# A GFNet token mixer and a SiLU feed-forward block in one kernel: row stores moved from ScalarE's queue to SyncE's, the last rows fetched group by group, one batch's first input laid on 128 partitions, its results stored before other stores, and the weight conversion cut into other pieces

## The chip, the cores and the metric

The kernel runs on one core of one Trainium2 chip. The metric is the device time of one execution in microseconds. Three runs of the kernel before took 2512.32, 2512.67 and 2513.15 us; the median is 2512.67 us.

The core has five engines, each with its own queue that is worked off in order: TensorE (PE, matmuls), VectorE (DVE), ScalarE (ACT), GpSimd (POOL) and SyncE (SP, which here only issues DMAs). DMAs are issued from the queues of SP, ACT and POOL. An engine that waits for a semaphore holds up everything behind it in its queue.

## The reference

```python
x: (8, 3008, 256)            # batch, tokens, channels
X = rfft(x, axis=1)          # over the tokens
y = irfft(X * F, n=3008)     # F = filt_r + i filt_i, per frequency and channel
h = y.reshape(24064, 256) @ w_in      # 256 -> 2048
out = silu(h) @ w_out                 # 2048 -> 256, silu(h) = h / (1 + exp(-h))
```

x, F and out are float32; w_in and w_out arrive as float64 and are turned into float32 on the core.

## The kernel before, in words

**The feed-forward part** makes up nearly all of the time. The tokens are worked off in 48 *pairs* of blocks, each with 8 *steps*: 384 steps in all. A step multiplies a pair's tokens with one 256-column slice of w_in (`hidden`), applies SiLU, and the step after multiplies the result with the matching slice of w_out (`project`). Both products use Strassen's scheme: seven matmuls in place of eight, for which sums of weights (S1, S2, S3, S4) stand beside the weight blocks A11, A12, A22. One step holds up to eight *rounds*. In its rounds `hidden` emits the matmuls A11 (round 0), A12 (1), S2 (2), S1 (3), S3 (4), A22 (6) and S4 (7); between them `project` emits the seven matmuls of the step before. TensorE takes them in that order.

On VectorE a step leaves this sequence: `g0` (A12's sum, after the matmul A12), then `finish` (two sums of the step before), later `g2` (after S3), `g1` (after S4), and, after a SiLU of ScalarE on `g1`, the wide sum `g46`. VectorE works it off in exactly this order: g1, g46 of one step, then g0 of the next, then finish. ScalarE copies the results of A11, S2 and S3 out of PSUM (`abc`) and applies the four SiLUs.

The steps are ordered so: pair 0 with weight slices 0, 1, 2 (steps 0 to 2), pair 1 with slices 0 to 7 (steps 3 to 10), then the rest of pair 0. So slice 1 is first used in step 1, slice 2 in step 2, slice 3 in step 6, slices 4 to 7 in steps 7 to 10.

**The weights** are prepared on the core. For each of 16 raw tiles j (two for each slice): `weights` loads it (512 KB, SP), `bits` takes exponent and mantissa words apart (VectorE, two instructions), `converted` makes the new exponent (ScalarE, two), `added` adds the low word, `signed` puts the sign back, `placed` multiplies both into `w_t` (VectorE, one each). `combine_weights(slice)` then makes the four sums with four VectorE additions: the first two (part 0) make S1 and S2, the other two (part 1) S3 and S4. `rounded` is added and signed together.

**The spectral part** of a batch is a mixed-radix transform in three stages of small matmuls, with two trips through DRAM (`d1` after stage 1, `d2` after the inverse of the middle stage). Batch 0 has to be done before any feed-forward step can start, so the kernel begins with a prologue: load batch 0, stage 1 (L392), `forward` (L526), filter products on VectorE and POOL, six inverse groups (`inverse_first`, L660), each evicted into two tiles q (`rows_first`, L678). Each q tile holds two halves of the token residues; the first halves are stored to d2 at once (`store_half(g, i, 0, ...)`, L684), by ACT for groups 0 to 3 and one tile each of groups 4 and 5, by SP for the other two. `load_t4_rows(k)` (L711) fetches 16 of the 48 rows each: k = 0 and 2 by SP, k = 1 by POOL. `stage3` (L726) then makes the first half of batch 0's tokens, y[0, 0], and L740 evicts it. Meanwhile stage 1 of batch 1 begins: `load_two` loads the first two pieces of its x on 96 partitions, `stage1` (L416) multiplies them and ACT copies them into the tiles t1 (L421). While the PE has to wait in this stretch, matmuls without a use (`idle`) are run.

Once y[0, 0] is there, a small POOL copy (`gate`, L1374) opens a series of POOL DMAs: the twelve second halves of the q tiles (L684), and then the eight stores of batch 1's t1 tiles to d1 (`store_rows`, L429). The tiles t1 come from a pool of two buffers, so the next piece of stage 1 (t1 of piece 2, copied by ACT in step 1) has to wait until the first piece's four stores have landed. SP loads the later weights and pieces of x.

**What orders the rest**: `put(step, round, piece)` writes each other piece of work into the engines' queues at a place given by step and round. The long table near the end (L1395 and on) places the weights' pieces in steps 0 to 9, `plan` places the spectral work of batches 1 to 7.

## Time and profile before

| what | us |
|---|---|
| median of the runs | 2512.67 |
| the profiled execution, its own time | 2514.95 |
| its span, first to last instruction | 2513.0 |
| TensorE busy in the span | 2484.8 |
| VectorE busy | 1760.7 |
| ScalarE busy | 1095.1 |
| POOL busy | 438.4 |
| prologue, until the first matmul of step 0 | 59.80 |

The first matmuls (A11) of steps 0 to 11 start at 59.80, 65.05, 81.73, 90.63, 98.46, 107.42, 115.35, 123.77, 130.85, 138.09, 144.43 and 151.78 us; a step later in the kernel lasts a little over 6 us plus what spectral work is put into it. The profiled execution is 2.28 us longer than the median of the runs, and 1.95 us of its time lie outside the span.

A line of the timeline gives the start, the time until the end of the group, the engine, the line of the kernel, the operation, what is written and read, the count, and in brackets the idle time before it and who ended it. A line of the chain gives the start, the length and the work. A matmul of 256 columns in float32 shows as two instructions.

### The profile page before, as it was taken

What the parts mean: (1) busy time and instruction counts of PE and PEld (TensorE: products, weight loads), DVE (VectorE), ACT (ScalarE), POOL (GpSimd) and SP (SyncE); (2) the same over time, 40 slices, a digit from 0 to 9 for tenths busy, and PEclk for the clock granted to TensorE, in tenths of its full rate; (3) what the DMA queues carried; (4) which work ended last, traced back from release to release, by engine and by line L of the source; (5) the groups of instructions that cost most, each with busy time, mean ns of one, the idle gap of its engine ahead of it and who ended that gap; (6) DMA issues with size and microseconds to landing.
All of it is one profiled execution on the core that took longest, in us unless ns stands there. A gap on an engine that the chain in (4) does not pass through costs nothing.

```text
span 2513.0 us, 42305 instructions
## 1 busy us (share of the span) xinstructions
PE 2484.8 (99%) x16238; PEld 2127.2 (85%) x16238; DVE 1760.7 (70%) x3608; ACT 1095.1 (44%) x3006; POOL 438.4 (17%) x687
## 2 busy tenths in 40 slices
PE   8899999999999999999999999999999999999999
PEld 6678888888888888888888888888888888888988
DVE  6766777777777777777777767777677766655544
ACT  3544444444444444444444444444444444444443
POOL 3202212022121121210222112211122111101100
PEclk9999999999999999999999999999999999999999
DMA  7522242312333132420324203331042211200000
GB/s 256 191 72 90 65 101 52 87 51 67 73 72 83 35 80 60 100 71 19 93 58 111 60 26 77 86 74 43 26 107 62 55 43 34 63 21 9 17 9 17
DMA packets 139513, 170.67 MB, mean 68 GB/s; under 512 B 21084, under 2 KB 113084, under 8 KB 138684
## 3 DMA queue, kind: packets, MB, share of 16 engines
q1 hardware_dynamic: 115408, 120.23, 18.2%
q0 software_dynamic: 22816, 46.20, 7.0%
q8 instruction: 127, 2.08, 0.3%
q10 hardware_dynamic: 1088, 1.56, 0.2%
q14 instruction: 74, 0.61, 0.1%
HBM read 96.06 MB, written 81.26 MB: 71 GB/s over the span
## 4 chain that ended last, share of the span: by engine, by line
PE 96%; DVE 2%; DMA 1%; ACT 0%; issue 0%; POOL 0%; SPq 0%; DVEq 0%; ACTq 0%
PE acc L1057 45%; PE px L989 25%; PE pyz L989 19%; PE pd L764 1%; PE pf L486 1%; PE pc L582 1%; PE pb L544 1%; DVE g L960 1%; PE pc L660 0%; PE pa L392 0%; PE pd L726 0%; PE pb L526 0%; DMA d<-t 0%; DMA d<-q 0%; DMA w_t<-d 0%
## 5 line engine op out<-in xcount | busy, mean ns | idle before, releaser
L1057 PE MATMUL acc<-g,w_t 128*128 128x256 f32 (+1 forms) x5376 | 1508.5, 376 | 3.0 <-ACT o L777 2.5
L1057 PEld LDWEIGHTS acc<-g,w_t 128*128 128x128 f32 x5376 | 1016.6, 190 | 154.6 <-ACT o L777 15.3
L960 DVE TENSOR_TENSOR g<-pyz,abc 128x256 f32<-128x256 f32 (+1 forms) x1152 | 479.6, 416 | 481.5 <-ACT abc L1010 240.7
L960 DVE TENSOR_TENSOR g<-g 128x256 f32<-128x256 f32 (+3 forms) x1152 | 590.6, 513 | 196.6 <-ACT g L993 183.4
L989 PE MATMUL px<-ty,w_t 128*128 128x256 f32 (+1 forms) x2304 | 676.6, 375 | 7.7 <-ACT abc L1010 7.7
L993 ACT ACTIVATE g<-g 128x256 f32<-128x256 f32 (+1 forms) x1152 | 472.9, 411 | 241.5 <-DVE g L960 241.5
L989 PEld LDWEIGHTS px<-ty,w_t 128*128 128x128 f32 x2304 | 434.2, 190 | 65.4 <-ACT abc L1010 8.9
L960 POOL TENSOR_TENSOR s<-s 128x256 f32<-128x256 f32 (+1 forms) x322 | 246.3, 782 | 1387.3 <-DVE s L1083 1043.7
L989 PE MATMUL pyz<-y,w_t 128*128 128x256 f32 (+1 forms) x1536 | 452.4, 376 | 3.0 <-DVE g L960 2.6
L989 PEld LDWEIGHTS pyz<-y,w_t 128*128 128x128 f32 x1536 | 283.3, 189 | 49.0 <-DVE g L960 9.0
L1004 ACT COPY abc<-px 128x256 f32<-128x256 f32 (+1 forms) x384 | 141.4, 368 | 369.8 <-PE px L989 369.8
L1010 ACT COPY abc<-px 128x256 f32<-128x256 f32 (+1 forms) x384 | 141.5, 368 | 308.6 <-PE px L989 308.5
L993 ACT ACTIVATE g<-px 128x256 f32<-128x256 f32 (+1 forms) x384 | 145.8, 380 | 298.1 <-PE px L989 298.1
L989 PE MATMUL px<-y,w_t 128*128 128x256 f32 (+1 forms) x768 | 227.6, 378 | 0.5 <-ACT g L993 0.5
L989 PE MATMUL pyz<-ty,w_t 128*128 128x256 f32 (+1 forms) x768 | 225.6, 375 | 0.2 <-DVE g L960 0.2
L989 PEld LDWEIGHTS px<-y,w_t 128*128 128x128 f32 x768 | 143.8, 190 | 23.2 <-ACT g L993 2.2
L989 PEld LDWEIGHTS pyz<-ty,w_t 128*128 128x128 f32 x768 | 142.0, 190 | 21.5 <-DVE g L960 1.3
L997 ACT COPY abc<-px 128x256 f32<-128x256 f32 (+1 forms) x384 | 135.1, 352 | 35.5 <-PE px L989 35.5
L506 POOL DMA_DIRECT2D d<-tf x96 | 48.5, 505 | 215.8 <-DVE tf L436 212.9
L1083 ACT COPY s<-acc 128x512 f32<-128x512 f32 (+1 forms) x92 | 53.0, 577 | 46.4 <-issue 28.8
L603 POOL DMA_DIRECT2D d<-low x36 | 22.2, 618 | 289.1 <-DVE low L599 289.1
L476 DVE TENSOR_TENSOR uf<-x_all 120x512 f32<-120x512 f32 (+1 forms) x72 | 60.2, 864 | 0.0
(133 smaller groups left out, 1363.2 us busy)
## 6 DMA issues: line engine op xcount, KB each, us to landing
t<-d SPq DMA_DIRECT2D x84, 256.0 KB
t<-d SPq DMA_DIRECT2D x224, 96.0 KB
out_dram<-s SPq DMA_DIRECT2D x62, 256.0 KB
d<-q POOLq DMA_DIRECT2D x48, 256.0 KB, 5.2
x_all<-in_x_dram SPq DMA_DIRECT2D x96, 96.0 KB
x_all<-xr SPq DMA_DIRECT2D x96, 96.0 KB
d<-tf POOLq DMA_DIRECT2D x96, 96.0 KB, 2.7
d<-tq POOLq DMA_DIRECT2D x96, 96.0 KB, 2.8
```

The lines of the kernel that those rows point to most:

```text
L476: nc.vector.tensor_tensor(out=out, in0=in0, in1=in1, op=op)
L486: nc.tensor.matmul(out=ps[q][32 * k:32 * k + 32], lhsT=wq_t[rows, k], rhs=rhs[k][rows], start=True, stop=True)
L506: nc.gpsimd.dma_start(out=d1[par, :, grp, at:at + 4], in_=part[rows].rearrange("p q n c -> p (q n) c"))
L544: nc.tensor.matmul(out=ps[k, ri][32 * j:32 * j + 32, a, :], lhsT=dn_t[rows, 4 * (g + a) + at, :], rhs=t2s[g + a][rows, at, :], start=True, ...
L960: eng.tensor_tensor(out=out, in0=in0, in1=in1, op=op)
L989: nc.tensor.matmul(out=out, lhsT=w_t[:, jp, c, 0], rhs=rhs, start=start, stop=True, skip_group_check=True)
L993: nc.scalar.activation(out=g[:, k, 0:n], in_=g[:, k, 0:n] if src is None else src, func=AFT.Silu)
L997: nc.scalar.copy(out=sums[:, 0, 0:n], in_=xo)
L1004: nc.scalar.copy(out=sums[:, 1, 0:n], in_=xo)
L1010: nc.scalar.copy(out=sums[:, 2, 0:n], in_=xo)
L1057: nc.tensor.matmul(out=acc[pair][i][:, h, 0:n], lhsT=w_t[:, jp, OUT_PLACE.get(c, c), 1], rhs=g[:, k, 0:n], start=(new and h == 0), stop=la ...
L1083: copy(out=dst, in_=src)
```

## The change

1. **Row stores issued by SP.** Of the first-half stores, ACT issues one tile each of groups 0, 1, 2, 3 and 5; SP issues the other seven (five more than before). ACT now makes the copies of group 4 and one of group 5 with no issue between them.
2. **Last rows fetched by group.** `load_t4_rows` becomes `fetch_rows(a0, n, queue)`; the last 16 rows are fetched by SP in two portions of eight (rows 32 to 39 of group 4, then 40 to 47 of group 5), four DMAs of 128 KB in place of two of 256 KB.
3. **Batch 1's first x on 128 partitions.** `load_four` loads it in four DMAs onto 32 partitions each, with a contraction of three blocks of 32 rows; `stage1_four` multiplies it with twelve matmuls on four row groups in place of four on 96 rows. One of the four copies moves to VectorE. The table wx3 gets a tile of its own in another pool. The idle matmuls change from 24 small and 6 large ones to 9 and 12.
4. **t stored ahead of the halves.** The eight `store_rows` DMAs come before the twelve second halves in POOL's queue.
5. **The weights' pieces.** In the prologue, `added(0, 1)`, `bits(2, 3)` and `added(2, 3)` come earlier; tiles 7 to 10 are loaded in step 1. In the table, `rounded` is no longer used, combine_weights of slices 1, 2 and 3 is cut into its two parts, and the pieces move; the last one is in step 10 instead of step 9. One eviction of y (group 1) moves from ACT to VectorE, the token sums of pair 1 from round 3 to round 5 of step 2.

```diff
-        def load_two():
-            load_rows(x_all.rearrange("p i a n -> p (i a n)"), 0, 2)
+        def load_four():
+            xs["four"] = x_all.rearrange("p i a n -> p (i a n)")[:, 0:1536].rearrange("p (k n) -> p k n", k=3)
+            for q in range(4):
+                nc.sync.dma_start(out=xs["four"][32 * q:32 * q + 32],
+                                  in_=bass.AP(tensor=x.tensor, offset=x.offset + (b * S + 2 * q) * C,
+                                              ap=[[32 * C, 32], [32 * 32 * C, 3], [1, 2 * C]]))
+        def stage1_four():
+            ps = [bank(b, f"pa_{b}_{q}") for q in range(4)]
+            xt = xs.pop("four")
+            for k in range(3):
+                for q in range(4):
+                    rows = slice(32 * q, 32 * q + 32)
+                    nc.tensor.matmul(out=ps[q].rearrange("p n c -> p (n c)"), lhsT=wx3_t[rows, k], rhs=xt[rows, k],
+                                     start=(k == 0), stop=(k == 2), skip_group_check=True)
             for u in range(2):
-                xs[u] = x_t[u].rearrange("p a n -> p (a n)")
+                t1 = us["t1", u] = tpool.tile([128, 2, 2, C], FP32, name=f"t1_{b}_{u}", tag="t")
+                for h in range(2):
+                    (nc.vector.tensor_copy if u and h else nc.scalar.copy)(out=t1[:, h], in_=ps[2 * u + h])
...
-                copy, queue = (nc.scalar.copy, nc.scalar) if i == 0 or g < 4 else (nc.scalar.copy if g == 4 else nc.vector.tensor_copy, nc.sync)
-                copy(out=qt, in_=halves[g][i])
-                store_half(g, i, 0, queue)
+                last = g == NG - 1
+                (nc.vector.tensor_copy if last and i else nc.scalar.copy)(out=qt, in_=halves[g][i])
+                store_half(g, i, 0, nc.scalar if i == 0 and g != 4 else nc.sync)
...
-        def load_t4_rows(k, queue=None):
-            first, by = SPREAD[k]
+        def fetch_rows(a0, n, queue):
+            k, r0 = divmod(a0, 16)
             for h in range(2):
-                (queue or nc.sync).dma_start(out=us["t4"][64 * h + first:64 * h + first + 15 * by + 1:by],
-                                  in_=d2[0, 16 * k:16 * k + 16, :, h, :])
+                queue.dma_start(out=us["t4"][64 * h:64 * h + 64].rearrange("(q r) n c -> q r n c", r=4)[r0:r0 + n, k],
+                                in_=d2[0, a0:a0 + n, :, h, :])
...
-    part["load_t4_rows"](0)
-    part["load_t4_rows"](1, nc.gpsimd)
+    part["fetch_rows"](0, 16, nc.sync)
+    part["fetch_rows"](16, 16, gp)
     bits(0, 1)
     inverse(4)
+    added(0, 1)
     inverse(5)
+    part["fetch_rows"](32, 8, nc.sync)
+    part["fetch_rows"](40, 8, nc.sync)
+    bits(2, 3)
     converted(0, 1)
-    added(0, 1)
-    part["load_t4_rows"](2)
-    bits(2, 3)
-    converted(2, 3)
+    added(2, 3)
     signed(0, 1)
     placed(0, 1)
-    for u in range(2):
-        second["stage1"](u, False)
+    second["stage1_four"]()
+    converted(2, 3)
     combine_weights(0)
-    rounded(2, 3)
+    signed(2, 3)
     placed(2, 3)
-    idle(6, small=24)
+    idle(12, small=9)
     for g in range(4):
         part["stage3"](g)
     gp.tensor_copy(out=gate, in_=y[0, 0][:, 0, 28:29])
+    for u in range(2):
+        second["store_rows"](u)
     for g in (2, 3, 4, 5, 0, 1):
         for i in range(2):
             part["store_half"](g, i, 1, gp)
-    for u in range(2):
-        second["store_rows"](u)
...
-            (0, 1, (combine_weights, 1), (bits, 4)), (0, 5, (converted, 4), (bits, 5), (added, 4)),
-            (1, 0, (converted, 5), (weights, 8, 9, 10)), (1, 1, (signed, 4), (placed, 4), (rounded, 5), (placed, 5)),
-            (1, 3, (bits, 6), (added, 6)), (1, 5, (converted, 6), (combine_weights, 2)),
-            (2, 1, (signed, 6), (placed, 6), (bits, 7), (added, 7)), (2, 5, (converted, 7), (bits, 8), (weights, 11)),
...
-            (5, 3, (bits, 12), (added, 12)), (5, 5, (converted, 12), (combine_weights, 3), (weights, 15)),
-            (6, 1, (signed, 12), (placed, 12), (bits, 13), (added, 13)), (6, 3, (bits, 14)),
-            (6, 5, (converted, 13), (combine_weights, 4)),
-            (7, 0, (converted, 14)), (7, 1, (signed, 13), (placed, 13), (rounded, 14), (placed, 14)),
-            (7, 5, (combine_weights, 5)), (7, 7, (bits, 15)), (8, 0, (converted, 15)),
-            (8, 1, (rounded, 15), (placed, 15)), (8, 5, (combine_weights, 6)), (9, 5, (combine_weights, 7))):
+            (0, 1, (combine_weights, 1, 0)), (0, 5, (combine_weights, 1, 1), (bits, 4), (converted, 4)),
+            (1, 0, (weights, 7, 8)), (1, 1, (added, 4), (signed, 4), (placed, 4)), (1, 2, (weights, 9, 10)),
+            (1, 3, (bits, 5)), (1, 5, (converted, 5), (added, 5), (bits, 6)), (2, 0, (converted, 6)),
+            (2, 1, (signed, 5), (placed, 5), (combine_weights, 2, 0)), (2, 3, (combine_weights, 2, 1), (added, 6)),
+            (3, 1, (signed, 6), (placed, 6)), (3, 3, (bits, 7), (added, 7)),
+            (3, 5, (converted, 7), (bits, 8), (added, 8), (weights, 11)),
+            (4, 0, (converted, 8)), (4, 1, (signed, 7), (placed, 7), (signed, 8)), (4, 3, (placed, 8), (bits, 9)),
+            (4, 5, (converted, 9), (added, 9), (bits, 10), (weights, 12, 13)),
+            (5, 0, (converted, 10)), (5, 1, (signed, 9), (placed, 9), (added, 10)), (5, 3, (signed, 10), (placed, 10)),
+            (5, 5, (bits, 11), (added, 11)), (6, 0, (converted, 11), (weights, 14, 15)),
+            (6, 1, (combine_weights, 3, 0), (signed, 11), (placed, 11)), (6, 3, (combine_weights, 3, 1), (bits, 12)),
+            (6, 5, (converted, 12), (added, 12), (bits, 13)), (7, 0, (converted, 13)),
+            (7, 1, (combine_weights, 4), (signed, 12)), (7, 5, (placed, 12), (added, 13), (signed, 13)),
+            (8, 1, (combine_weights, 5), (placed, 13)), (8, 5, (bits, 14), (added, 14)), (9, 0, (converted, 14)),
+            (9, 1, (combine_weights, 6), (signed, 14)), (9, 5, (placed, 14), (bits, 15), (added, 15), (converted, 15)),
+            (10, 1, (signed, 15), (placed, 15), (combine_weights, 7))):
```

More of the change, by code (lines that the diff above doesn't have):

```diff
@@ L738, in stage3 @@
             for h in range(2):
-                copy = nc.vector.tensor_copy if g > 1 and h == 1 else nc.scalar.copy
+                copy = nc.vector.tensor_copy if g > 0 and h == 1 else nc.scalar.copy
                 copy(out=dst[:, :, h, :, n0:n0 + 4], in_=ps[h].rearrange("p a i n -> p a n i"))
@@ L794, in fold_wide @@
                 nc.vector.tensor_tensor(out=dst[:, :, :, at:at + n], in0=even[:, :, :, 0:n], in1=odd[:, :, :, 0:n], op=op)
-        return dict(us=us, store_half=store_half, store_rows=store_rows, evict_y=evict_y, halves=halves, load_first=load_first, stage1_first=stage1_first, load_x=load_x, load_two=load_two, stage1=stage1, reverse_x=reverse_x,
+        return dict(us=us, store_half=store_half, load_four=load_four, stage1_four=stage1_four, store_rows=store_rows, evict_y=evict_y, halves=halves, load_first=load_first, stage1_first=stage1_first, load_x=load_x, stage1=stage1, reverse_x=reverse_x,
                     load_fold=load_fold, fold=fold, stage1_fold=stage1_fold, evict_fold=evict_fold, pairs_fold=pairs_fold, forward_two=forward_two, free_two=free_two, multiply_two=multiply_two, add_two=add_two, inverse_two=inverse_two, even_two=even_two, rows_two=rows_two, ends_two=ends_two,
-                    load_t2=load_t2, forward=forward, multiply=multiply, add=add, inverse=inverse, inverse_first=inverse_first, rows_first=rows_first, even=even, rows=rows, load_t4=load_t4, load_t4_rows=load_t4_rows, stage3=stage3,
+                    load_t2=load_t2, forward=forward, multiply=multiply, add=add, inverse=inverse, inverse_first=inverse_first, rows_first=rows_first, even=even, rows=rows, load_t4=load_t4, fetch_rows=fetch_rows, stage3=stage3,
                     load_wide=load_wide, stage3_wide=stage3_wide, copy_wide=copy_wide, turn_wide=turn_wide, fold_wide=fold_wide)
@@ L1269, in placed @@
                 load_exact(j)
-    wx3_t = qpool.tile([128, 2, C], FP32, name="wx3", tag="q").rearrange("p a c -> p (a c)")[:, 0:384].rearrange(
-        "p (k m) -> p k m", k=3)
+    wx3_t = upool.tile([128, 3, 128], FP32, name="wx3", tag="u")
     nc.sync.dma_start(out=wx3_t, in_=wx3_dram.ap())
@@ L1311 @@
     nc.sync.dma_start(out=wi_t, in_=ws_dram.ap())
-    second["load_two"]()
+    second["load_four"]()
     weights(0, 1, 2, 3, 4, 5)
@@ L1384 @@
     second["load_x"](3)
-    weights(7)
     early[0] = None
@@ L1395 @@
     for step, rnd, *todo in (
-            (0, 1, (combine_weights, 1), (bits, 4)), (0, 5, (converted, 4), (bits, 5), (added, 4)),
-            (1, 0, (converted, 5), (weights, 8, 9, 10)), (1, 1, (signed, 4), (placed, 4), (rounded, 5), (placed, 5)),
-            (1, 3, (bits, 6), (added, 6)), (1, 5, (converted, 6), (combine_weights, 2)),
-            (2, 1, (signed, 6), (placed, 6), (bits, 7), (added, 7)), (2, 5, (converted, 7), (bits, 8), (weights, 11)),
-            (3, 0, (converted, 8)), (3, 1, (signed, 7), (placed, 7), (added, 8)), (3, 3, (signed, 8), (placed, 8)),
@@ L1401 @@
-            (3, 5, (bits, 9), (added, 9), (weights, 12)),
-            (4, 0, (converted, 9), (weights, 13)), (4, 1, (signed, 9), (placed, 9), (bits, 10), (added, 10)),
-            (4, 3, (bits, 11), (added, 11)), (4, 5, (converted, 10), (weights, 14)),
-            (5, 0, (converted, 11)), (5, 1, (signed, 10), (placed, 10), (signed, 11), (placed, 11)),
-            (5, 3, (bits, 12), (added, 12)), (5, 5, (converted, 12), (combine_weights, 3), (weights, 15)),
-            (6, 1, (signed, 12), (placed, 12), (bits, 13), (added, 13)), (6, 3, (bits, 14)),
@@ L1420 @@
     for pair in range(len(pairs)):
-        step, rnd = combines[pair % per] if pair not in (1, 2) else ((2, 3), (11, 5))[pair - 1]
+        step, rnd = combines[pair % per] if pair not in (1, 2) else ((2, 5), (11, 5))[pair - 1]
         pending.append((pair // per * STEPS + step + rnd / ROUNDS, 98, lambda pair=pair: tokens(pair)))
```

## The prediction

> **What bounds the kernel now.** The page says first that TensorE carries it: it is busy for 99% of the span and holds 96% of the chain that ended last. Only stretches where TensorE waits can give anything, or be made longer. The chain in order of time, asked for the first 100 us, shows where they are:

> ```profile
> 42.83 2.52 DMA d<-w_t
> 45.41 0.56 SPq L711
> 46.02 5.95 DMA w_t<-d
> 52.22 3.66 PE pd L726 x126
> 55.91 2.35 PE pd L726 x123
> ...
> 59.70 7.18 DMA d<-q
> 68.75 1.37 POOL d L429 x3
> 70.28 7.18 DMA d<-t
> ```

> There are two. The prologue's stage 3 (L726) waits for the last rows from d2. And the stores of batch 1's t tiles stand in POOL's queue behind the second halves, and land at 77.46. The timelines of ScalarE and TensorE show whom that holds up (in brackets the idle time before, and who ended it):

> ```profile
> 77.60 1.07 ACT L421 COPY t<-pa 128x512 f32<-128x512 f32 x2 [9.40 <-DMA d<-t]
> 79.00 1.22 PE L989 MATMUL px<-ty,w_t 128*128 128x256 f32 x2 [7.22 <-ACT abc L1010]
> ```

> ScalarE cannot write t1 of piece 2 before the old tile is stored, `abc` stands behind that copy, and TensorE behind `abc`: 7.22 us in step 1. The table by stage adds the granted clock (the third number from the right) and the DMAs:

> ```profile
> 46.00:50.00 4.00, 1.14 (x11) 0.95 (x9) 3.84 (x8) 3.93 (x8) 0.10 (x1) 0.94 0.84 219
> 50.00:52.00 2.00, 0.42 (x2) 0.28 (x2) 2.00 (x5) 0.72 (x2) 0.00 (x0) 0.50 0.33 90
> 72.00:78.00 6.00, 0.00 (x0) 0.00 (x0) 0.59 (x1) 0.40 (x1) 1.50 (x3) 0.90 0.96 375
> 78.00:84.00 6.00, 5.00 (x13) 4.05 (x14) 2.97 (x7) 3.68 (x9) 1.97 (x4) 0.53 0.38 113
> ```

> After both waits TensorE runs at half clock: from 49.5 to 56.3 and from 76.8 to 83.7. Last, what VectorE does between two steps (step 4 to 5), and TensorE's matmul S2 beside it:

> ```profile
> 107.62 0.42 DVE L960 TENSOR_TENSOR g<-pyz,abc 128x256 f32<-128x256 f32 x1 [0.79 <-PE pyz L989]
> 108.53 0.69 DVE L960 TENSOR_TENSOR g<-g 128x512 f32<-128x512 f32 x1 [0.48 <-ACT g L993]
> 109.13 0.42 DVE L960 TENSOR_TENSOR g<-pyz,abc 128x256 f32<-128x256 f32 x1
> 109.47 0.88 DVE L960 TENSOR_TENSOR g<-g 128x256 f32<-128x256 f32 x2
> 110.26 0.68 DVE L1208 SCALAR_TENSOR_TENSOR e<-raw,e 128x512 uint32<-128x512 uint32 x1
> ```

> ```profile
> 107.42 0.59 PE L989 MATMUL px<-y,w_t 128*128 128x256 f32 x2
> 109.14 0.59 PE L989 MATMUL px<-ty,w_t 128*128 128x256 f32 x2
> ```

> g1, g46, g0, finish: the piece placed in round 1 starts only 2.63 us after g1, 2.84 us after A11 (107.42). TensorE issues S2 1.72 us after A11.

> **The change part by part**, against the profiled execution (2514.95 us, 2513.0 of it span); differences carry over to the median, 2512.67.

> *Row stores and last rows.* ACT sheds five issues of 0.46 us, SP takes them. SP's order in the changed program is: four stores, rows 0 to 15 (two issues of 0.6), three stores (0.55 each), then the four small fetches. The fourth store waits for a slot that the last raw weight load frees, 38.87 by ACT's store of now; so SP is at the fetches of rows 0 to 15 at 39.4 (now 39.05) and through its last store at 42.4. POOL's fetch, which waits for that fourth store, can go at 41.3 (now 44.73). The first small fetch waits for group 4's stores, which lie behind rows 0 to 15 in SP's own queue: landed about 44.9 (now 45.35 for the last two). Four issues at 0.6 put the last at 46.7, now 46.02. From there the shortest landing in this stretch is 2.52 us (49.2, a gain of 2.8), the longest 5.95 (52.65, a loss of 0.7). The nearest row is the long one, the same rows into the same tile, with POOL's 512 KB beside it, which will now be mostly done; I take 51.2, a gain of 0.8. [...]

> VectorE has added(0, 1) (1.28) in its gap before 40.38, then 1.28 us more work than now (two y and t copies); it ended at 53.18 and next worked at 57.33, so that is covered; without cover it is 1.28.

> *First x on 128 partitions.* Same 768 KB in four issues; twelve matmuls go at 10.83/96 = 0.113 us for each of their 24 instructions, 2.7 us in place of 3.70, the idle ones at about 3.4 in place of 3.0. All of it lies before TensorE's wait for the rows: 0. Bounds: 1 us either way if the rows came by 47. ACT's first store now waits for a quarter of x (the whole landed at 30.28); behind it ACT waits for POOL until 30.84 anyway.

> *t stored first.* The gate moves with the prologue. Eight POOL issues of 0.5 us, the first four through 2.2 us after the gate; at the worst landing, 7.18, the first tile is free by 68, and ACT's copy comes at 70: no wait. The halves are late next: POOL's queue, then SP's loads of tiles 7 to 10, which wait for the q tiles of groups 2 and 3, then pieces of x behind them. Four more issues, 7.2 to land, 7.2 for the load: 82 at worst, and bits 7 is due about 88. Step 1 becomes an undisturbed one: 14 matmuls at 0.43 and one stage-1 piece at 1.72 are 7.75, and 0.21 for ACT's conversion ahead of the SiLU (step 2 lost as much): 7.96 against 16.68 now (65.05 to 81.73). **-8.72.**

> *The pieces, step 0.* Now bits 4 is in round 1 and its conversion finds it ready. In the changed order VectorE does g2 (63.16), half of combine(1) (0.73), then bits 4, so its first word is ready at 64.65 instead of 63.15; ACT converts (1.44) ahead of the SiLU on A22, and A11 of step 1 follows 0.42 after that SiLU's start: 66.5 instead of 65.05. **+1.45.**

> *The pieces, steps 2 to 10.* combine(2) to combine(7) now stand in the step whose S2 needs them; before, all ended half a step earlier, and S2 never waited for VectorE. In the order of the changed program S2 of steps 2, 6, 7, 8, 9 and 10 waits for it. Part 0 starts 2.88 us after A11 at the earliest, takes 0.77 (half of 1.54), and a weight load precedes the matmul by 0.27: S2 3.92 us after A11, not 1.72, and 0.11 for the restart: 2.31. In steps 2 and 10 signed and placed (0.72 + 0.61) stand before it. Against an undisturbed step (7.75 in steps 2 to 6, 6.03 in 7 to 9, 7.35 in step 10 with its stage 3, as now): step 2 +3.43 (A11 comes 0.21 late there, so the wait is that much less); step 3 +0.21; step 4 +0.69 (drains of pair 0 delay g1, now 0.8 and 0.19); step 5 0; step 6 +2.52; step 7 +2.10; step 8 +2.74 (placed 12, added 13, signed 13, 1.93 in all, delay g1 by 0.43); step 9 +2.31 and +1.64, because conversion 15 waits for bits 15 placed in the same round; step 10 +3.46. The steps are 11.18, 7.96, 8.44, 7.75, 10.27, 8.13, 8.77, 9.98, 10.81: 83.29 us. Now they take 70.05 (81.73 to 151.78), of which 5.9 are waits for VectorE, ACT and the clock. **+13.24.**

> *The clock.* TensorE now idles 3.3 us before S2 in steps 2 and 10. After 2.34 us of idling (47.14) the clock fell, after 71.8 only 4.9 us later; so each gap may drop it. A drop that lasts 4.6 us under work, as from 79.0, costs 2.3. Bounds 0 and 4.6; half of one, **+1.15**, taken. [...]

> Sum: -0.8 - 8.72 + 1.45 + 13.24 + 1.15 = +6.3. 2512.67 + 6.3 = **2519**.

> **The rivals.**
> - *The combine stays off the path (faster).* If VectorE reaches part 0 before TensorE needs it, the S2 waits (16.35 in all, restart included) and the clock's share go; what remains is that steps 7 to 9 hold more VectorE work than fits, some 1.8 us: 2519 - 16.35 - 1.15 + 1.8 = 2503.3. It decides once the six waits sum to less than 4.4 us. For it: VectorE is 70% busy. Against: the chain above is latency, not load; the gap before g46 is 0.48 in nearly every step. 0.12.
> - *The prologue gives more (no change).* Rows at 49.2, and TensorE's gap short enough to keep the clock: 2.8 and 1.2 (stage 3 took 5.98, at the fast half's 2.35 per 123 it takes 4.85) instead of 0.8, no drop later: 2512.67 + 5.17 - 3.2 = 2514.6. For it: POOL's fetch leaves early. Against: 46.7 is late. 0.22.
> - *The clock drops at every long gap.* Two drops at 2.3 and one in a shorter gap: 2517.8 + 6.9 = 2524.7. 0.13.
> - *The t stores are still late*, as the DMAs stay at 0.9 to 1.0 from 60 to 78: half of the wait, 3.6 us, remains: 2522.6. Against: nothing is ahead of them in POOL's queue. 0.05.
> - The likeliest, 0.48: its own range 2515 to 2522.

> **How the numbers follow.** 0.2% (5 us, 2507.6 to 2517.7) is about what a measurement of this kernel can tell from no change. Faster: the first rival, 0.12. Same: the second, 0.22, and three tenths of the likeliest, 0.14. Slower: 0.52. Leaving out the fast rival and the upper end of the clock's, the range is 2510 to 2524.

> **What would show it.** In the profile after: no wait of ACT for `d<-t`, and step 1 at 8 us; waits of TensorE's `px<-ty` for DVE `w_t` (L960 of now) of 2 to 3.3 us in steps 2, 6, 7, 8, 9, 10, 12 to 14 us idle in all; A11 of step 11 about 5 us later than 151.78; ScalarE's conversion in step 0 waiting for bits; the last fetch landing at 51. The prediction is wrong if the waits before S2 are under 1 us, if stage 3 starts before 49.5, or if half clock shows in more than one of steps 2 to 10.

## The result, and the profile after

The changed kernel takes 2528.59 us (median of 6 runs), the kernel before 2512.95 us beside it: ratio 1.0064, 95% interval 1.0051 to 1.0077. It is slower by 15.6 us, where +6.3 was forecast.

All of it lies in the first 166 us. The first matmuls (A11) of the steps start so in the two profiled executions:

| step | 0 | 1 | 2 | 3 | 4 | 5 | 6 | 7 | 8 | 9 | 10 | 11 |
|---|---|---|---|---|---|---|---|---|---|---|---|---|
| before | 59.80 | 65.05 | 81.73 | 90.63 | 98.46 | 107.42 | 115.35 | 123.77 | 130.85 | 138.09 | 144.43 | 151.78 |
| after | 61.13 | 67.99 | 76.03 | 90.23 | 99.26 | 107.29 | 115.16 | 125.34 | 133.55 | 143.88 | 155.31 | 166.28 |

From step 11 to the end of the span both need 2361.1 to 2361.2 us (2513.0 - 151.78 and 2527.4 - 166.28). So A11 of step 11 measures the whole change in one profile: +14.5 us. (The medians are 15.6 apart, since the profiled execution of before was 2.0 above its median and that of after 0.6.)

The chain that ended last, in the prologue of after (start, length, work):

```profile
41.91 5.38 DMA d<-q
47.29 0.02 SPq L727
...
47.34 0.84 SPq L727
...
48.24 0.74 SPq L727
...
49.10 3.33 DMA w_t<-d
...
53.68 6.73 PE pd L742 x237
```

A first-half store takes 5.4 us to land, and only then can SP issue the first small fetch, at 47.34; before, the last fetches went at 45.41. Stage 3 (L742) ends at 60.4, before at 58.3.

TensorE's waits in the timeline of after (idle time and who ended it in brackets), and ScalarE's copy into t1 of piece 2:

```profile
67.99 0.70 PE L1005 MATMUL px<-y,w_t 128*128 128x256 f32 x2 [2.14 <-ACT g L1009]
81.31 1.19 PE L1005 MATMUL px<-ty,w_t 128*128 128x256 f32 x2 [3.29 <-DVE w_t L976]
99.26 0.70 PE L1005 MATMUL px<-y,w_t 128*128 128x256 f32 x2 [1.03 <-ACT g L1009]
119.06 0.67 PE L1005 MATMUL px<-ty,w_t 128*128 128x256 f32 x2 [2.00 <-DVE w_t L976]
129.16 0.67 PE L1005 MATMUL px<-ty,w_t 128*128 128x256 f32 x2 [1.83 <-DVE w_t L976]
137.80 0.81 PE L1005 MATMUL px<-ty,w_t 128*128 128x256 f32 x2 [2.06 <-DVE w_t L976]
147.74 0.67 PE L1005 MATMUL px<-ty,w_t 128*128 128x256 f32 x2 [1.97 <-DVE w_t L976]
155.31 0.70 PE L1005 MATMUL px<-y,w_t 128*128 128x256 f32 x2 [1.32 <-ACT g L1009]
160.58 0.67 PE L1005 MATMUL px<-ty,w_t 128*128 128x256 f32 x2 [3.28 <-DVE w_t L976]
```

```profile
72.61 0.59 ACT L437 COPY t<-pa 128x512 f32<-128x512 f32 x1 [1.47 <-PE pa L432]
```

ScalarE no longer waits for the t stores (before: 9.40 us). In its place stand the six waits for VectorE's `w_t` that were forecast, 14.43 us in all, and three waits for a SiLU. How the wait in step 10 comes about, on VectorE:

```profile
156.97 0.42 DVE L976 TENSOR_TENSOR g<-pyz,abc 128x256 f32<-128x256 f32 x1 [0.39 <-PE pyz L1005]
157.32 0.88 DVE L976 TENSOR_TENSOR g<-g 128x256 f32<-128x256 f32 x2
158.11 0.68 DVE L1224 SCALAR_TENSOR_TENSOR e<-raw,e 128x512 uint32<-128x512 uint32 x1
158.83 0.69 DVE L1231 SCALAR_TENSOR_TENSOR w_t<-m,e 128x512 f32<-128x512 f32 x1
159.55 1.55 DVE L976 TENSOR_TENSOR w_t<-w_t 128x256 f32<-128x256 f32 x4
```

g0, finish, signed, placed, and only then the sums of which the second is S2: TensorE, ready at 157.3, starts S2 at 160.58.

The table by stage has the granted clock third from the right:

```profile
82.00:84.00 2.00, 2.00 (x7) 1.53 (x5) 0.43 (x1) 0.69 (x2) 0.00 (x0) 0.50 0.95 379
...
138.00:140.00 2.00, 2.00 (x6) 1.62 (x6) 0.92 (x2) 0.69 (x2) 0.00 (x0) 0.55 1.13 213
...
148.00:150.00 2.00, 2.00 (x7) 1.64 (x7) 0.87 (x2) 0.69 (x2) 0.00 (x0) 0.61 0.00 0
```

Behind three of the waits, in steps 2, 8 and 9, TensorE works at half clock. Two of these gaps are of 2.06 and 1.97 us.

### The profile page after: what moved, and what is told of

It is laid out like the page before. It is cut to its first block, busy times and chain, and to the rows that moved or that the text cites. A ratio compares the mean times of both kernels' runs of the same rounds, so it can differ in the third digit from the quotient of the medians.

```text
span 2527.4 us, 42323 instructions
## 1 busy us (share of the span) xinstructions
PE 2489.5 (98%) x16236; PEld 2130.5 (84%) x16236; DVE 1762.2 (70%) x3610; ACT 1095.8 (43%) x3004; POOL 438.7 (17%) x687
## 4 chain that ended last, share of the span: by engine, by line
PE 96%; DVE 2%; ACT 1%; DMA 0%; issue 0%; POOL 0%; SPq 0%; DVEq 0%; ACTq 0%
PE acc L1073 45%; PE px L1005 26%; PE pyz L1005 19%; PE pd L780 1%; PE pf L502 1%; PE pc L598 1%; PE pb L560 1%; DVE g L976 1%; PE pc L676 0%; PE pd L742 0%; PE pa L432 0%; PE pa L392 0%; PE pb L542 0%; PE pc L656 0%; DVE w_t L976 0%
## 5 line engine op out<-in xcount | busy, mean ns | idle before, releaser
L1005 PE MATMUL px<-ty,w_t 128*128 128x256 f32 (+1 forms) x2304 | 677.6, 376 | 15.1 <-DVE w_t L976 14.4
```

What stands on the lines that cost most here:

```text
L1005: nc.tensor.matmul(out=out, lhsT=w_t[:, jp, c, 0], rhs=rhs, start=start, stop=True, skip_group_check=True)
```

## The experiments

Each run is read by its time and by its step lengths. Ratios are against the kernel before on the same chip, with 95% intervals.

**1. The t stores first, and nothing else.** On the kernel before:

```diff
+    for u in range(2):
+        second["store_rows"](u)
     for g in (2, 3, 4, 5, 0, 1):
         for i in range(2):
             part["store_half"](g, i, 1, gp)
-    for u in range(2):
-        second["store_rows"](u)
```

> The kernel before with one edit: the eight stores of batch 1's t tiles stand ahead of the twelve second halves. Theory A (the gain of part 4 is real and stands by itself; the loss came with the table of weight pieces and the prologue): step 1 falls from 16.68 us to 8 to 11, the more the pieces of tiles 4 to 6 (4.7 us of VectorE in that step of before) now stand in its way; the drop of the clock at 76.8 goes; A11 of step 0 stays at 59.8; time 2504 to 2507. Rival B (part 4 only pays with the new table, since tile 7's load is now late): VectorE waits for raw 7 at bits 7 of step 2 for 3 to 6 us; 2509 to 2513.

Measured: 2505.14 us against 2514.16, ratio 0.9966 (0.9953 to 0.9978). Step 1 is 8.47 us in place of 16.68, step 2 8.69 in place of 8.90, and steps 3 to 10 are the same within 0.1 each. No half clock from 58 to 94 us. A11 of step 0 came at 58.58, where 59.8 was expected, though nothing ahead of it was changed. Theory A holds; the gain of this one part stands by itself and needs nothing of the new table.

**2. The new prologue with the old table.** The changed kernel with before's table, tile 7's load and token sums' place:

```diff
     second["load_x"](3)
+    weights(7)
...
-            (0, 1, (combine_weights, 1, 0)), (0, 5, (combine_weights, 1, 1), (bits, 4), (converted, 4)),
+            (0, 1, (combine_weights, 1), (bits, 4)), (0, 5, (converted, 4), (bits, 5), (added, 4)),
...
-        step, rnd = combines[pair % per] if pair not in (1, 2) else ((2, 5), (11, 5))[pair - 1]
+        step, rnd = combines[pair % per] if pair not in (1, 2) else ((2, 3), (11, 5))[pair - 1]
```

> The changed kernel with the kernel before's table of pieces, its place of tile 7's load and of pair 1's token sums. Theory A (the table costs 20 us in steps 2 to 10, the prologue 1.3): as the run with t first alone, plus 1.3 us of prologue (A11 of step 0 at 61.1): 2505 to 2508, no wait of TensorE for VectorE's w_t in steps 2 to 10. Rival (the prologue's change is what upsets the steps, by what it leaves late): A11 of steps 2 to 10 keep lengths of 9 to 11 us, and the time stays above 2520.

Measured: 2507.72 us, ratio 0.9973 (0.9963 to 0.9983). A11 of step 0 at 60.93; steps 0 to 10 within 0.1 us of those of experiment 1. So the table, with the two places moved along with it, makes the loss: 2528.59 against 2507.72.

**3. Matmuls without a use in the waits.** On the changed kernel, ahead of S2, seven in steps 2 and 10 and four in steps 6 to 9 (`FILL = {2: 7, 6: 4, 7: 4, 8: 4, 9: 4, 10: 7}`):

```diff
+        if step in FILL:
+            ps = fps.tile([128, 2, C], FP32, name=f"fill_{step}", tag="f")
+            for _ in range(FILL[step]):
+                nc.tensor.matmul(out=ps[:, 0], lhsT=wx_t, rhs=wide_rows, start=True, stop=True)
         mm(xo, S2, t[:, 2, 0:n], False)
```

> The changed kernel with matmuls without a use (0.43 us each) ahead of S2: seven in steps 2 and 10, four in steps 6 to 9, so that TensorE works through most of the wait for the combined weights. The six waits keep their length. Theory A (the waits cost twice: 14.4 us of idling and, in three of them, a drop of the clock that costs 6.0): no half clock in steps 2, 8, 9; those steps are 3.0, 1.6 and 1.5 us shorter; A11 of step 11 at 160.3 in place of 166.3; time 2521 to 2524. Rival C (the longer steps have another cause, such as VectorE's order or DMA traffic, and the low clock only stands beside it): the steps keep their lengths, 2527 to 2530. If each filled step pays for the filler, up to 0.3 us each, 1.8 more.

Measured: 2523.18 us, ratio 1.0038 (1.0023 to 1.0053). Steps 2, 8 and 9 are 11.39, 8.65 and 9.90 us: 2.81, 1.68 and 1.53 less than in the first profile of after. The unfilled steps 3 to 5 and the filled 6, 7 and 10 keep their lengths within 0.02. So the low clock was a price of its own, 6.0 us, beside the waits:

```profile
79.44 3.19 PE L1022 MATMUL fill<-d_t,wx_t 96*128 96x256 f32 x14
82.89 0.67 PE L1005 MATMUL px<-ty,w_t 128*128 128x256 f32 x2 [0.26 <-DVE w_t L976]
```

S2 of step 2 still starts about 5.3 us after A11, with 0.26 us of idling left. One thing was not as expected: step 1 is 9.73 us (8.04 in the profile of after), at half clock from 68 to 72. Up to there the two programs are the same. The wait of 2.14 us at the end of step 0, which had cost nothing more in the first profile, drops the clock here.

**4. Part 0 of the combine half a step earlier,** for slices 3 to 6 of the changed kernel:

```diff
-            (5, 5, (bits, 11), (added, 11)),
-            (6, 1, (combine_weights, 3, 0), (signed, 11), (placed, 11)),
+            (5, 5, (combine_weights, 3, 0), (bits, 11), (added, 11)),
+            (6, 1, (signed, 11), (placed, 11)),
...
-            (7, 1, (combine_weights, 4), (signed, 12)),
+            (7, 1, (combine_weights, 4, 1), (signed, 12)),
...
```

Part 0 of slices 4, 5 and 6 goes to (6, 5), (7, 5) and (8, 5); part 1 stays where the whole was.

> The changed kernel with one edit: the first part of combine_weights of slices 3 to 6 stands half a step earlier (round 5 of the step before). Theory A (the waits before S2 come from the place of the combine): the waits for w_t in steps 6 to 9 go (7.86 us and four restarts of 0.11), and with them the clock drops of steps 8 and 9 (3.0): about 11 us less, 0 to 2 of them given back where the two additions (0.77) in round 5 delay g1; those of steps 2 and 10 stay; 2517 to 2520. Rival D (VectorE is simply full in these steps, so the wait moves to another of its results): the S2 waits go, but waits for g or pyz take their place and the time stays above 2524.

Measured: 2524.05 us, ratio 1.0042 (1.0027 to 1.0057). By the time alone this would be Rival D, by the steps it is theory A. Steps 6 to 9 are 8.68, 6.65, 7.25 and 8.49 us: 9.1 less than after's. The four waits for `w_t` are gone, and 1.74 us of waits for `g` came in their place:

```profile
116.93 0.70 PE L1005 MATMUL pyz<-y,w_t 128*128 128x256 f32 x2 [0.48 <-DVE g L976]
132.60 0.70 PE L1005 MATMUL pyz<-y,w_t 128*128 128x256 f32 x2 [0.83 <-DVE g L976]
139.45 0.70 PE L1005 MATMUL pyz<-y,w_t 128*128 128x256 f32 x2 [0.43 <-DVE g L976]
146.49 0.70 PE L1005 MATMUL px<-y,w_t 128*128 128x256 f32 x2 [1.48 <-ACT g L1009]
151.77 1.19 PE L1005 MATMUL px<-ty,w_t 128*128 128x256 f32 x2 [3.28 <-DVE w_t L976]
```

What hid the gain is the clock at waits that were not touched: step 1 is 1.7 us longer than in the first profile, and step 10 15.33 in place of 10.97, at half clock from 151 to 161.

**5. Two conversions a round later,** on the changed kernel:

```diff
-            (0, 5, (combine_weights, 1, 1), (bits, 4), (converted, 4)),
-            (1, 0, (weights, 7, 8)),
+            (0, 5, (combine_weights, 1, 1), (bits, 4)),
+            (1, 0, (converted, 4), (weights, 7, 8)),
...
-            (9, 5, (placed, 14), (bits, 15), (added, 15), (converted, 15)),
+            (9, 5, (placed, 14), (bits, 15), (added, 15)),
+            (10, 0, (converted, 15)),
```

> The changed kernel with one edit: the conversions of tiles 4 and 15 stand one round later than their bits (rounds (1, 0) and (10, 0) in place of (0, 5) and (9, 5)). Theory A (a conversion in the round of its own bits holds ScalarE, and with it the SiLU that TensorE waits for): step 0 is 5.3 us in place of 6.9, step 9 about 1.5 us shorter, and the drop of the clock in step 1 that two of three runs with this start showed goes; the waits before S2 stay: 2523 to 2526. Rival (ScalarE only fills a wait that VectorE's bits impose anyway): steps 0 and 9 keep their lengths, 2527 to 2530.

Measured: 2526.74 us, ratio 1.0048 (1.0033 to 1.0063), between the two forecasts. Step 0 is 4.55 us in place of 6.86, step 9 9.94 in place of 11.43, and both waits for the SiLU are gone: theory A. The six waits for `w_t` stay (3.29, 2.01, 1.83, 2.06, 1.98, 3.43), and this time steps 6, 8, 9 and 10 have the low clock and step 2 has not (11.39).

**6 to 8. The prologue's parts,** each undone alone on the kernel of experiment 2. The last rows in one portion:

```diff
-    part["fetch_rows"](32, 8, nc.sync)
-    part["fetch_rows"](40, 8, nc.sync)
+    part["fetch_rows"](32, 16, nc.sync)
```

> The changed kernel with the kernel before's table, and the last sixteen rows fetched in one portion (two DMAs in place of four, after group 5's stores). Theory E (small portions cost: four issues of 0.75 us one after the other, and 3.3 us to land): the two issues end about 48.7 in place of 50.5; if their landing takes 3.3 as for the small ones, stage 3 starts about 1 us earlier, A11 of step 0 at 60. Theory F (the last stores land late, at 47.3, whatever is fetched after them; sixteen rows in one take 5 to 6 us to land, as in the kernel before): rows at 53.5 to 54.5, A11 of step 0 at 61.5 to 63.

The stores issued as before:

```diff
-                last = g == NG - 1
-                (nc.vector.tensor_copy if last and i else nc.scalar.copy)(out=qt, in_=halves[g][i])
-                store_half(g, i, 0, nc.scalar if i == 0 and g != 4 else nc.sync)
+                copy, queue = (nc.scalar.copy, nc.scalar) if i == 0 or g < 4 else (nc.scalar.copy if g == 4 else nc.vector.tensor_copy, nc.sync)
+                copy(out=qt, in_=halves[g][i])
+                store_half(g, i, 0, queue)
```

> The changed kernel with the kernel before's table, and the first-half stores issued as before (nine by ACT, SP two of groups 4 and 5; rows still fetched by group). Theory G (part 1 costs: group 4's second store stands behind the fetch of rows 0 to 15 in SP's queue): the first small fetch goes at 45 in place of 47.35, and A11 of step 0 about 2 us earlier than with SP's stores, 59. Theory H (the stores of groups 4 and 5 are slow since the early fetch by POOL moves 512 KB beside them): POOL's fetch goes at 44 to 45 again as in the kernel before, the stores land at 45.4, and the last rows come then with POOL's 512 KB beside them: 51.5 to 53, A11 59.5 to 60.5. Rival I (part 1 costs nothing): all as with the old table alone, A11 at 60.9.

POOL's fetch held back:

```diff
-    part["fetch_rows"](16, 16, gp)
...
     inverse(5)
+    gp.tensor_copy(out=gate, in_=part["us"]["q", 5][1][:, 0, 0:1])
+    part["fetch_rows"](16, 16, gp)
```

> The changed kernel with the kernel before's table, and POOL's fetch of rows 16 to 31 held back until group 5's second copy is done (a copy of one column on POOL reads it): about 43.5 in place of 41.3. Theory H (POOL's early fetch makes the last stores slow): the first small fetch goes before 46, at the price of 512 KB beside the last rows; A11 of step 0 within 1 us of 60.9 either way. Theory G (it is the place of the store in SP's queue): the first small fetch stays at 47.3, the POOL rows land later, A11 at 61 to 63.

| | POOL's fetch | first fetch of the last rows | stage 3's last wait ends | A11 of step 0 | time | ratio (95%) |
|---|---|---|---|---|---|---|
| 2: new prologue | 42.42 | 47.35 | 53.46 | 60.93 | 2507.72 | 0.9973 (0.9963 to 0.9983) |
| 6: one portion | 43.28 | 47.64 | 52.30 | 59.78 | 2505.13 | 0.9965 (0.9952 to 0.9978) |
| 7: stores as before | 43.42 | 45.38 | 52.41 | 59.96 | 2506.33 | 0.9967 (0.9955 to 0.9980) |
| 8: POOL late | 46.81 | 45.59 | 54.17 | 61.60 | 2508.43 | 0.9976 (0.9966 to 0.9987) |

The intervals of the four times overlap, so they don't tell the four apart; what follows rests on the profiles, one of each. Theory E fits: in experiment 6 the fetches go 0.3 us later, and the rows are there 1.2 us earlier. From the first fetch to the end of the last wait it is 4.7 us, against 6.1 to 6.6 in the six profiles with four small fetches that start step 0 at about 61 (the changed kernel and experiments 2, 3, 4, 5 and 10). The busy share of the 16 DMA engines, in tenths, from 47 to 54 us in 40 slices, with the four small fetches (experiment 2), then with two large ones (experiment 6):

```profile
DMA  8452100000024552155344444544344420000000
```

```profile
DMA  8997741100015489999999974200004000000000
```

The small ones never fill more than about half of the engines: 1 to 5 tenths from 48.9 us on. The large ones take 9 tenths in the eight slices from 49.6 to 51.0 us.

On the stores, theory H's forecasts were met in experiments 7 and 8, theory G's only in part (the first fetch at 45 in experiment 7, but not A11 at 59; in experiment 8 the fetch did not stay at 47.3). Experiment 8 leaves SP's order as it was and only takes POOL's 512 KB away: group 4's store then lands in 4.03 us (4.78 in experiment 2) and the first fetch goes 1.76 us earlier. So the traffic beside the store is part of the delay, as theory H has it. It isn't shown to be all: 1.0 of the 1.76 us come from an earlier start of that store (41.51 against 42.52), and where ACT issues the stores as before, the store that the fetch waits for lands in 2.1 to 3.2 us (before, experiments 1, 7 and 11). And POOL's rows then land last (5.51 us in the chain), so nothing is won:

```profile
41.51 4.03 DMA d<-q
45.53 0.02 SPq L727
45.59 0.85 SPq L727
...
47.33 5.51 DMA w_t<-d
```

**9. The changed kernel once more, unchanged.**

> The changed kernel once more, unchanged, for a second profiled execution. Theory A (a wait of 1.8 us and more is only a chance of a clock drop, which depends on where the gap falls; each drop costs about 1.7 us): the same seven waits (2.1 us at the end of step 0, six before S2) with the same lengths, but half clock in another set of steps; step lengths differ from the first profile by about 1.7 up or down in those steps and by under 0.2 elsewhere. Rival (the drops belong to certain steps, by something that the program does there): the same three steps, 2, 8 and 9, with the same lengths.

One run: 2532.50 us. The nine waits shown above are the same to 0.01 us but for one (0.92 in place of 1.32 ahead of step 10), and the low clock is in six steps in place of three. Those that the first profile had not, steps 1, 6 and 10:

```profile
66.00:68.00 2.00, 2.00 (x7) 1.62 (x6) 1.22 (x3) 0.37 (x1) 1.48 (x3) 0.57 0.34 133
...
118.00:120.00 2.00, 2.00 (x6) 1.50 (x5) 1.24 (x4) 0.11 (x1) 0.00 (x0) 0.50 0.00 0
...
162.00:164.00 2.00, 2.00 (x34) 1.26 (x34) 0.00 (x0) 0.00 (x0) 0.00 (x0) 0.50 0.00 0
```

Steps 1, 2, 6, 8, 9 and 10 are 9.72, 12.93, 11.88, 10.33, 11.03 and 15.29 us long (first profile: 8.04, 14.20, 10.18, 10.33, 11.43, 10.97). Theory A holds for steps 1, 6 and 10; but steps 8 and 9 show the drop in both, which is also what its rival expected of them; the part on why the prediction was wrong comes back to them. And A11 of step 0 came at 58.56, 2.6 us earlier than in the first profile.

**10. Tile 7's conversion two rounds later,** on the changed kernel (`(converted, 7)` from (3, 5) to (3, 7)).

> The changed kernel with one edit: the conversion of tile 7 goes two rounds later in step 3, behind the last SiLU of that step. Theory A (in step 3 ScalarE's queue holds the drain copy of pair 0 and the conversion, 1.44, ahead of the SiLU that step 4's first matmul waits for): the wait of 1.03 us goes and step 3 is 7.9 to 8.1 us in place of 9.03. Rival (the drain copy, or VectorE's sums, hold the SiLU anyway): step 3 stays at 8.7 or above. The time as a whole within 3 us of the changed kernel's, by the clock's chance.

One run: 2533.37 us, with the low clock in steps 1, 2, 8, 9 and 10. Step 3 is 7.83 us in place of 9.03, so the cause was right; but step 4 is 10.04 in place of 8.03, and the time is 4.8 us above the changed kernel's median, where at most 3 were expected (0.9 above experiment 9). Tile 7's conversion now stands in step 4, ahead of the `abc` that S2 waits for, and tile 8's right behind that `abc`:

```profile
101.45 0.70 PE L1005 MATMUL pyz<-y,w_t 128*128 128x256 f32 x2 [0.63 <-DVE g L976]
103.52 0.70 PE L1005 MATMUL px<-ty,w_t 128*128 128x256 f32 x2 [0.94 <-ACT abc L1013]
```

**11. Parts 1, 2 and the table undone together** (experiments 6 and 7 in one).

> The changed kernel with parts 1, 2 and 5's table undone: stores issued as before, the last rows in one portion, the table of before; the t stores first and x on 128 partitions stay. If the two prologue terms (1.0 and 1.15 on the first matmul of step 0) add, that matmul starts at 58.8 and the time is 2503 to 2505. If they are the same microsecond (both wait for POOL's 512 KB), it starts at 59.8 and the time is that of either alone, 2505 to 2506.5.

Measured: 2504.62 us, ratio 0.9963 (0.9949 to 0.9977). A11 of step 0 at 57.60, earlier than either forecast (by less than the 2.6 us by which the unchanged program scattered), and steps 1 to 10 as in experiment 1. It beats both kernels, and by its time can't be told from experiment 1 (2505.14), which is one moved loop.

**12. The sums of slices 3 to 7 on POOL,** on the kernel of experiment 11:

```diff
-            (3, 5, (bits, 9), (added, 9), (weights, 12)),
+            (3, 5, (bits, 9), (added, 9), (weights, 12), (combine_weights, 3, None, gp)),
...
-            (5, 5, (converted, 12), (combine_weights, 3), (weights, 15)),
+            (5, 5, (converted, 12), (weights, 15), (combine_weights, 5, None, gp)),
...
```

Slices 4, 6 and 7 go to (4, 5), (7, 5) and (8, 5).

> The version before this one, with combine_weights of slices 3 to 7 on POOL (idle there but for DMA issues) in place of VectorE, half a step to two steps ahead of their use. Theory J (with t first, VectorE's load is what sets steps 1 to 9: about 78 us of work in steps that take 78): 5 times 1.54 us leave VectorE, steps 4 to 9 (45.98 us with t first alone) take 42 to 44, TensorE's waits for VectorE's g in steps 6 to 8 go; 2500 to 2503. Rival K (POOL's additions are slow or disturb VectorE, or come too late for S2): waits for w_t in steps 6 to 10 and 2505 or more.

Measured: 2507.30 us, ratio 0.9971 (0.9960 to 0.9982). No wait for `w_t`, but steps 4 to 9 take 48.06 us in place of 45.94. VectorE's `added` in step 3, without and with POOL's sums beside it, and those sums:

```profile
88.00 0.69 DVE L1219 SCALAR_TENSOR_TENSOR m<-raw,m 128x512 f32<-128x512 uint32 x1
```

```profile
88.08 1.52 DVE L1219 SCALAR_TENSOR_TENSOR m<-raw,m 128x512 f32<-128x512 uint32 x1
```

```profile
88.31 3.72 POOL L976 TENSOR_TENSOR w_t<-w_t 128x256 f32<-128x256 f32 x4
```

Rival K, by the disturbance, not by lateness. VectorE's instructions with two inputs from SBUF get longer beside POOL's sums: between 88 and 132 us the one `added` beside them takes 1.52 us and the other six 0.68 to 0.69, and three of the four wide sums g46 that start while they run take 0.99 to 1.26 us in place of 0.69. The sums `g<-pyz,abc`, with one input from PSUM, keep theirs (416 ns in the mean without, 418 with).

## Why the prediction was wrong

The direction and most of the mechanisms were right; the sum was +6.3 and A11 of step 11 shows +14.5 (+17.8 in the second profile, experiment 9). By its own steps, in the first profile:

| term | forecast | measured | by |
|---|---|---|---|
| prologue | -0.8 | +1.33 | A11 of step 0 |
| step 0 | +1.45 | +1.61 | its length |
| step 1 (t stored first) | -8.72 | -8.64 | its length |
| steps 2 to 10, waits and queues | +13.24 | +14.2 | 90.25 - 70.05, less the next row |
| clock | +1.15 | +6.0 | steps 2, 8, 9 over their forecast lengths (3.02, 1.56, 1.45); experiment 3 |

**The t stores first, step 0, and the six waits were right.** 16.68 us became 8.04 (7.96 forecast), and experiment 1 shows the gain alone. The waits sum to 14.43 us without restarts; steps 5, 6, 7 and 10 came within 0.2 us of their forecast lengths. The prediction's step 10 was 0.18 us short of its own terms (2.31 + 0.72 + 0.61 make 3.64, not 3.46); with them it comes to 10.99, and 10.97 was measured. Experiment 4 shows that the place of part 0 makes the waits of steps 6 to 9, and experiment 5 that the same-round conversions make the waits in steps 0 and 9.

**The clock is the step that failed.** The prediction took "half of one" drop, by the gaps of 3.3 us in steps 2 and 10, and gave several drops a chance of 0.13. It left out the gaps of 2 us, though it had itself named a fall after 2.34 us of idling. In the four profiles whose waits before S2 were untouched (both of after, experiments 5 and 10) the low clock follows the gap of step 8 (2.06 us) and of step 9 (1.97) each time, of steps 2 and 10 (3.3) three times, of step 6 (2.00) twice, and of step 7 (1.83) never. The rival that came nearest was "the clock drops at every long gap", 2524.7.

What decides it can be read from the traces. Within each profile all changes of the granted clock stand at multiples of 3.41 us from each other, at another place in each run (first profile, from the first fall at 49.45 us to 151.85: 10.24, 20.48, 6.83, 51.20, 3.41, 6.83 and 3.41 us apart). Cut into windows on this grid, the 14 profiles have 493 windows between 58 and 190 us that run at full clock. Behind the 23 of them in which TensorE idles 1.92 us or more, the next window has half clock, every time; behind the 470 with 1.91 us or less, none has. (The bound holds for this stretch: in the prologue of experiment 1, where small matmuls run, the clock fell behind a window with 1.22 us of idling.) So what counts is how much of a gap falls into one window. The most idle time that one window holds at each wait, in us (bold where half clock followed):

| wait in step | length, first profile | changed kernel | experiment 9 | experiment 10 | experiment 5 |
|---|---|---|---|---|---|
| 0 (end) | 2.14 | 1.47 | **2.14** | **2.15** | no wait |
| 2 | 3.29 | **2.15** | **2.97** | **2.64** | 1.76 |
| 6 | 2.00 | 1.34 | **2.01** | 1.90 | **2.01** |
| 7 | 1.83 | 1.21 | 1.05 | 1.77 | 1.35 |
| 8 | 2.06 | **2.06** | **2.06** | **1.92** | **2.06** |
| 9 | 1.97 | **1.97** | **1.97** | **1.98** | **1.98** |
| 10 | 3.28 | 1.91 | **2.19** | **2.54** | **3.17** |

The waits of steps 8 and 9 fell whole, or all but whole, into one window in all four profiles, and they stand about 10 us apart, near three windows, so that they are nearly one draw. Two waits of 3.3 us cost nothing more because the border between two windows cut them (1.91 and 1.42 us of idling on its two sides, and 1.76 and 1.53).

A drop lasts whole windows. Most last one, 3.41 us, and cost 1.5 to 1.8 us. That of step 2 lasts two in the first profile and in experiment 10 (6.83 us; it costs 2.8 and 3.1), where 1.14 and 0.64 us of the wait reached into the low window; 0.44 us in experiment 4 did not prolong it. That of step 10 lasts three in experiments 9 and 4 (10.24 us; 4.3 and 4.4), where 1.10 and 1.03 us reached into the first low window and stage 3's 64 small matmuls stand in the second, in which TensorE counts as busy throughout. What holds the clock down there was not shown.

Half of one window, 1.7 us, is about the common price, and one program shows its drops in other steps from run to run (2, 8 and 9 in the first profile, 1, 2, 6, 8, 9 and 10 in the second). That each gap may drop the clock, as the prediction has it, was right, and which of them does hangs on where the windows fall, as the table shows; the error was to take half of one draw for what are six. (The wait of 1.83 us in step 7 can't reach 1.92 by itself.) An estimate from these rows: if a drop needs 1.9 us of the gap inside one window, as the windows above have it, a gap of 2.0 meets it in (3.41 + 2.0 - 3.8)/3.41 = 47% of the positions, one of 2.14 in 51%, one of 3.3 in 85%; three, one and two of them at 1.7 us make 3 x 0.8 + 0.87 + 2 x 1.45 = 6.2 us. The first profile of after has 6.0; the second, summed in the same way, about 12, since every gap but that of step 7 dropped the clock there and step 10's drop cost 4.3.

**The prologue's term was mis-sized, with the wrong sign.** Its step was "landed about 44.9", the store that SP's first small fetch waits for. It landed at 47.3, and the four issues behind it took 3.1 us (0.78 each, not 0.6). POOL's fetch did go early, at 41.32 (41.3 forecast), but its 512 KB were not "mostly done": they ran beside these stores (DMA share 0.92 to 1.02 from 42 to 46 us). Experiment 8 shows that this is part of the delay (group 4's store lands in 4.03 us in place of 4.78); the rest stays open. Undoing part 1 or part 2 brings A11 back by 1.0 or 1.2 us, both together by 3.3. That sum isn't additive, and it has to be read with the scatter: of the seven profiles with this prologue six start step 0 at 60.92 to 61.22, and the second one of the unchanged program at 58.56; the kernel before and experiment 1 start it at 59.80 and 58.58. In the early one SP's fetch of rows 0 to 15 went at 38.16, in the other six at 38.51 to 40.53; but the one with 38.51, experiment 5, started step 0 at 60.92, so what makes the early start stays open.

**Step 3** was 1.07 us over its forecast: ScalarE's queue held the drain of pair 0 and the conversion of tile 7 ahead of a SiLU. The prediction had +0.21 there, the figure that it gave a conversion ahead of the SiLU in step 1; +1.28 was measured. Experiment 10 shows the cause, and that moving it gives nothing.

The rival by which the combine stays off the path fell with the six waits, and the one of late t stores with ScalarE's line above.

**x on 128 partitions** was forecast at 0. No run undid it alone; with it (experiment 11) and without it (experiment 1) the times can't be told apart.

Of the conditions named for being wrong, the one met was the third: half clock in more than one of steps 2 to 10.

## What to carry to other kernels

Price an idle gap of TensorE twice: its length, and the chance that it costs a window of half clock behind it; here gaps of 1.97 to 2.06 us did so in 10 of 12 cases, at some 1.7 us each, and six such gaps are not half of one. Ask how much of a gap can fall into one window: less than 1.9 us never cost anything between 58 and 190 us here, and filling the gaps (experiment 3) kept the clock at 1.00 in the steps that were filled. A sum that the next matmul needs belongs half a step ahead of it; the latency of what stands before it on VectorE is paid in full, however idle that engine is on the whole (14.43 us in six waits here, with VectorE busy for 70% of the span). When a transfer is started earlier, ask which transfer that something waits for it will run beside: POOL's earlier fetch ran beside the very stores that gate the last rows, and delayed them (4.78 us to land beside it, 4.03 without).
